# The lead-in of a fused linear-attention and gated-FFN kernel: wider state matmuls, other fillers, and w_in in six pieces

## Chip, cores, metric

The kernel runs on one core of a Trainium2 chip. The metric is the device time of one execution in microseconds; the median of ten runs is given where no other run is named. A single profiled execution gives the trace.

## What is computed

Linear attention with a decay per head over blocks of 64 positions, and then a feed-forward layer with a cosine gate on the 3,072 tokens that come out of it. Inputs are float32: q, k and v are [4, 8, 768, 64] (batch, heads, positions, head size), w_in is [512, 2048], w_out [2048, 512].

```python
for b in range(nb):                       # blocks of 64 positions
    intra = einsum('bhic,bhjc->bhij', qb, kb) * Dmask
    intra = einsum('bhij,bhjd->bhid', intra, vb)
    inter = einsum('bhid,bhde->bhie', qb * lam_pow, kv_state)
    out[:, :, sl] = intra + inter
    kv_state = lam_block * kv_state + einsum('bhsd,bhse->bhde', kb * rev_pow, vb)
x = out.transpose(0, 2, 1, 3).reshape(3072, 512)
h = x @ w_in
result = (h * cos(h)) @ w_out
```

## The kernel before

Positions are handled in tiles of 128 tokens, two tiles (a pair) at a time for attention. Tokens are grouped for the FFN in nine groups (`TILES`, 2 or 4 tiles each). For each group there are 16 blocks of 128 hidden columns: four matmuls per block (`hidden`, L707), a cosine on ScalarE (L713), a product on VectorE (L719); then a projection per tile of 16 matmuls, in groups of four (`project`, L751). While TensorE works through the FFN of one group, it does the attention of a later pair: scores (L420), state update (L432), values (L481), carried state (L509).

The first two pairs are different: two spans of 256 positions are loaded each by one DMA with the positions interleaved (`add_span`, L551). Per span, with two halves of four heads each: products of q and k with powers of lambda (L565, on VectorE, the second span's k on GpSimd), transposes on TensorE (L573) and copies on ScalarE (L576), scores (L584) masked by VectorE (L589), one state update per span (`update`, L592), whose two halves ScalarE copies into a block-diagonal bf16 tile (`update_out`, L602), values (L611), carried state (L617), and a copy of the result into xT (L625), which is the FFN's input.

In `update` TensorE makes, for each pair of heads p and each half s of the positions, two matmuls: head 2p into partitions 0 to 63 of one PSUM bank, head 2p+1 into 64 to 127 of another. That is 16 matmuls of 64x64 per span.

The order of work on every engine is set ahead of time by a list scheduler (`Planner`, L55): each task has an engine, an estimated duration, dependencies, a priority and a number of PSUM banks, and tasks are emitted in the planned order of starts. It sets only the order; at run time each engine goes through its instructions in that order and waits for semaphores. Loads go through two queues: SP (q, k, v, stores) and GpSimd (the two v spans, w_in, w_out, with a cast to bf16). Their order is the string `ORDER`; `i0` to `i4` are pieces of w_in, whose widths in blocks of 128 columns are `W_IN`, `o0` to `o3` are quarters of w_out. Piece 3 of w_in waits for the first masked scores of the second span (L307), and later loads wait for earlier ones (L793).

TensorE is kept busy in the lead-in by fillers that write a PSUM bank nobody reads: 94 matmuls of 64x32 at the very start (L841), and `keep_awake` (L830), called ahead of each planned TensorE task of the lead-in, which fills the planned gap with float32 matmuls on a zero tile:

```python
def keep_awake(us, at):
    cols = int((us - 0.06) * (1200.0 if at < 7.0 else 2400.0) / 4) // 64 * 64
    while cols > 0:
        n = min(cols, 4 * P)
        nc.tensor.matmul(idle_ps[:, :n], lhsT=blank[:, :P], rhs=blank[:, :n], start=True, stop=True)
        cols -= n
```

Of the kernel before, what the change touches and what calls it, by code (L numbers as in the profile page):

```python
# [10 lines left out]
F32 = mybir.dt.float32  # L11
# [20 lines left out]
VALUES_OUT = [("ACT", "ACT"), ("DVE", "ACT")]  # L32
STATE_OUT = [("ACT", "ACT"), ("ACT", "ACT")]
LATE = 30.0
AHEAD = 94
ORDER = "q0 k0 q1 k1 v0 v1 i0 i1 i2 i3 i4 o0 o1 o2 q4 q5 k4 k5 o3"

W_IN = [2, 2, 4, 4, 4]


class Task:
# [101 lines left out]
def kernel(  # L143
# [10 lines left out]
    nc = tc.nc  # L154
    B, H, S, D = q.shape
    P = 128
    NB = S // P
    NBLK = B * NB
    NP = H // 2
# [22 lines left out]
    def bank(i, shape, dt, name):  # L182
        return psum.tile(shape, dt, tag=f"bank{i}", bufs=1, name=name)
# [6 lines left out]
    ident = consts.tile([P, P], BF16)  # L190
# [20 lines left out]
    kv_bd = consts.tile([P, 2, NP, P], BF16)  # L211
# [29 lines left out]
    pl = Planner({**BUFS, "q_f": BUFS["ld"], "k_f": BUFS["ld"], "v_f": BUFS["ld"]})  # L241
# [3 lines left out]
    halves = [slice(i * D, (i + 1) * D) for i in range(2)]  # L245
# [20 lines left out]
    def start(queue, o, x, deps):  # L266
        i = queue.dma_start(out=o, in_=x)  # L267
        for d in deps:
            tc.add_manual_dep(i.ins, d.issue.ins.ins.name, mybir.DependencyInfo(
                mybir.DependencyClass.Sync, mybir.DependencyReason.DATA), reason="order of loads")  # L270
        return i
# [30 lines left out]
    def add_w(which, c, prio, deps=()):  # L302
        def emit(_):
            if which == "in":
                a, z = sum(W_IN[:c]) * P, sum(W_IN[:c + 1]) * P
                i = start(nc.gpsimd, w_in_sb[:, :, a:z], w_in_src[:, :, a:z], deps)
# [7 lines left out]

        part = W_IN[c] / 4 if which == "in" else 1.0
        early = which == "in" and c < 3
# [4 lines left out]
    T, So, Vo, d_t, Uo, Uo_sp = ({} for _ in range(6))  # L321
# [226 lines left out]
    spans, span_deps = [], []  # L548
    span_v = [consts.tile([P, H, 2, D], BF16, name=f"v_sp{x}") for x in range(SPANS)]

    def add_span(x):  # L551
        pa = lambda part: -1000.0 + 2 * x + part
        pv = lambda part: -990.0 + 2 * x + part
        cut = [slice(4 * hp, 4 * hp + 4) for hp in range(2)]
        us = {"DVE": 0.69, "POOL": 1.04}
        vec = {"DVE": nc.vector, "POOL": nc.gpsimd}
        L = {name: consts.tile([P, 2, H, D], BF16, name=f"{name}_sp{x}") for name in ("q", "k")}
# [32 lines left out]
                                        mask_sp.unsqueeze(1).to_broadcast([P, 2, 2, P]))  # L590

        def update(t):  # L592
            L["kv"] = [bank(i, [P, NP, D], F32, "ps_kv") for i in t.bank]
            rows = chunks[0][0]
            for p in range(NP):
                for s in range(2):
                    for i, h in enumerate(halves):
                        nc.tensor.matmul(L["kv"][i][h, p, :], lhsT=L["k"][rows, s, 2 * p + i, :], rhs=L["v"][rows, s, 2 * p + i, :],
                                         start=(p == 0 and s == 0), stop=True, skip_group_check=True)

        def update_out(_, h, e):
            (nc.scalar.copy if e == "ACT" else nc.vector.tensor_copy)(kv_bd[h, x, :, h], L["kv"][h.start // D][h])  # L602

        def values(task, hp):
            if hp == 0:
# [23 lines left out]
        so, kt, v_t = [[], []], [], [load_t["v_f", "sp", x]]  # L629
        for hp in range(2):  # L630
# [6 lines left out]
            for name, src in (("qT", a), ("kT", kt[hp])):  # L637
                e = OUTS[x][name][hp]
                t = pl.add("PE", MM(P, 4), [src, s_first if name == "kT" else None], partial(transposes, name=name, hp=hp), pa(-0.5 + 0.1 * hp), banks=1)
# [9 lines left out]
            if x and hp == 0:  # L649
                w_late.append(so[hp][0])  # L650

        u = pl.add("PE", 0.42, v_t + kt + [spans[0].get("carried")], update, pv(0.1), banks=2)
        Uo_sp[x] = [pl.add(e, 0.4 if e == "ACT" else 0.42, [u], partial(update_out, h=h, e=e), pv(0.1))
                    for h, e in zip(halves, STATE_OUT[x])]
        u.bank_frees = [[t] for t in Uo_sp[x]]
        span_deps.extend(v_t + kt)
        v0 = pl.add("PE", 0.35, so[0] + v_t + [spans[0].get("carried")], partial(values, hp=0), pv(0.2), banks=2)
        v1 = pl.add("PE", 0.35, [v0] + so[1], partial(values, hp=1), pv(0.25))
# [32 lines left out]
    def add_ffn(i):  # L691
# [4 lines left out]
        for f in range(KF):  # L696
            gate[f] = []
            blocks = [(0, 2), (2, 4)] if i == 0 and f < SPLIT else [(0, nb)]
            for b0, b1 in blocks:
# [16 lines left out]
                def gated(_, f=f, at=at, n=n):  # L716
                    if ("g", i) not in live:
# [3 lines left out]

                h = pl.add("PE", MM(n, 4), [x for m in range(n0 + b0, n0 + b1) for x in Vo[m]] + [w_t["in", next(c for c in range(len(W_IN)) if f < sum(W_IN[:c + 1]))]],
                           hidden, pr, banks=1)
# [59 lines left out]

    names = ORDER.split()
    for pr in range(SPANS, NBLK // 2):
# [18 lines left out]
    for x in range(SPANS):  # L804
        add_span(x)
# [22 lines left out]
    idle_ps = bank(idle.bank[0], [P, 4 * P], F32, "ps_idle")  # L828

    def keep_awake(us, at):  # L830

        cols = int((us - 0.06) * (1200.0 if at < 7.0 else 2400.0) / 4) // 64 * 64
        while cols > 0:
            n = min(cols, 4 * P)
            nc.tensor.matmul(idle_ps[:, :n], lhsT=blank[:, :P], rhs=blank[:, :n], start=True, stop=True)  # L835
            cols -= n

    for i in range(AHEAD):  # L841
        h = halves[i % 2]
        nc.tensor.matmul(idle_ps[h, :D // 2], lhsT=ident[h, :D], rhs=ident[h, :D // 2],
                         start=True, stop=True, skip_group_check=True)

    now = 4.2
    for t in plan:
        if t.eng == "PE" and t.start < lead_end.start + 1e-6:
            keep_awake(t.start - now, now)
            now = t.end  # L850
        if t.emit:
            t.ins = t.emit(t)
# [30 lines left out]
```

## Time and profile before

| | |
|---|---|
| median of 10 runs | 207.33 us (206.83 to 207.49) |
| profiled execution | 207.66 us |
| its span, first to last instruction | 206.0 us |
| TensorE: matmuls, busy | 2598, 198.9 us (97%) |
| VectorE, ScalarE, GpSimd busy | 55%, 58%, 31% |
| granted TensorE clock | 1.0 in all 40 slices |
| last span of the lead-in loaded (k of the second) | 11.04 us |
| first FFN matmul; FFN without pause from | 15.90 us; 17.44 us |

In the profile, PE stands for TensorE's matmuls, PEld for its weight loads, DVE for VectorE, ACT for ScalarE, POOL for GpSimd, SP for the queue of SyncE. L707 is line 707 of the kernel. A row of a timeline has the start, the duration and then the group of equal instructions; a bracket at its end gives the idle time before it and what ended that. A row of waits has the waiting group, what it waited for, then the total in us, how often, and the longest. A row by stretch has the stretch, its length, each engine's busy time with the number of its instructions, the granted clock, the share of the DMA engines and GB/s. In the list of DMA queues a row has packets, MB and the share of sixteen engines; q0 is GpSimd's queue, q1 that of SP, q8 and q14 carry instructions.

### The profile page before, as it was taken

What the parts mean: (1) busy time and instruction counts of PE and PEld (TensorE: products, weight loads), DVE (VectorE), ACT (ScalarE), POOL (GpSimd) and SP (SyncE); (2) the same over time, 40 slices, a digit from 0 to 9 for tenths busy, and PEclk for the clock granted to TensorE, in tenths of its full rate; (3) what the DMA queues carried; (4) which work ended last, traced back from release to release, by engine and by line L of the source; (5) the groups of instructions that cost most, each with busy time, mean ns of one, the idle gap of its engine ahead of it and who ended that gap; (6) DMA issues with size and microseconds to landing.
All of it is one profiled execution on the core that took longest, in us unless ns stands there. A gap on an engine that the chain in (4) does not pass through costs nothing.

```text
span 206.0 us, 6189 instructions
## 1 busy us (share of the span) xinstructions
PE 198.9 (97%) x2598; PEld 121.1 (59%) x2598; DVE 113.3 (55%) x221; ACT 119.0 (58%) x232; POOL 63.9 (31%) x84
## 2 busy tenths in 40 slices
PE   6999999999999999999999989999999999999993
PEld 5767444547747848666658756755454444444463
DVE  2688774256943947558467664735688444444001
ACT  5878772128837868466649476654778555354120
POOL 5856004056053364617254442524500000000000
PEclk9999999999999999999999999999999999999999
DMA  4999999998899999999996988988900110111112
GB/s 123 315 192 206 205 192 210 176 206 217 192 254 147 283 218 259 226 188 252 207 279 148 254 170 184 225 200 195 202 0 3 54 51 0 51 51 54 51 73 80
DMA packets 96379, 33.95 MB, mean 165 GB/s; under 512 B 84320, under 2 KB 93408, under 8 KB 96352
## 3 DMA queue, kind: packets, MB, share of 16 engines
q1 hardware_dynamic: 89376, 28.78, 62.1%
q0 software_dynamic: 6832, 4.72, 15.7%
q8 instruction: 20, 0.33, 0.6%
q10 hardware_dynamic: 144, 0.07, 0.1%
q14 instruction: 7, 0.06, 0.1%
HBM read 27.27 MB, written 6.29 MB: 163 GB/s over the span
## 4 chain that ended last, share of the span: by engine, by line
PE 77%; DMA 15%; SPq 3%; POOL 2%; issue 1%; DVE 1%; ACT 0%; POOLq 0%; ACTq 0%
PE ps_f L751 35%; PE ps_h L707 34%; DMA w_out_sb<-in_moe_w_out_dram 6%; DMA v_f<-in_v_dram 3%; DMA sp_f<-in_k_dram 3%; SPq L267 3%; PE ps_o L481 2%; DMA k_f<-in_k_dram 2%; PE ps_kv L432 2%; PE ps_o L509 1%; PE ps_s L420 1%; POOL w_in_sb L267 1%; POOL k_sp L565 1%; DVE v_s L350 0%; POOL w_out_sb L267 0%
## 5 line engine op out<-in xcount | busy, mean ns | idle before, releaser
L719 DVE TENSOR_TENSOR g<-ps_h,cos 128x256 bf16<-128x256 f32 (+1 forms) x148 | 72.9, 503 | 52.0 <-ACT cos L713 51.0
L713 ACT ACTIVATE cos<-ps_h,halfpi 128x256 f32<-128x256 f32 (+1 forms) x148 | 75.7, 538 | 32.3 <-PE ps_h L707 32.0
L751 PE MATMUL ps_f<-w_out_sb,g 128*128 128x512 bf16 (+2 forms) x416 | 92.4, 363 | 0.8 <-issue 0.8
L707 PE MATMUL ps_h<-xT,w_in_sb 128*128 128x256 bf16 (+1 forms) x592 | 91.8, 304 | 0.0
L707 PEld LDWEIGHTS <-w_in_sb 128*128 128x128 bf16 x592 | 57.3, 98 | 30.6 <-DVE xT L517 0.4
L751 PEld LDWEIGHTS <-g 128*128 128x128 bf16 x416 | 38.3, 98 | 36.7 <-issue 1.2
L765 ACT COPY o_sb<-ps_f 128x512 f32<-128x512 f32 (+1 forms) x24 | 13.8, 573 | 30.2 <-PE ps_f L751 30.2
L342 POOL TENSOR_TENSOR qk<-q_f,q_scale 128x512 bf16<-128x512 f32 x19 | 19.6, 1043 | 36.7 <-DMA q_f<-in_q_dram 28.7
L350 POOL TENSOR_TENSOR v_s<-v_f,v_scale 128x512 bf16<-128x512 f32 x19 | 19.7, 1042 | 19.5 <-DMA v_f<-in_v_dram 17.2
L517 ACT CAST xT<-ps_o 128x512 bf16<-128x512 f32 x19 | 10.2, 588 | 11.5 <-PE ps_o L509 9.0
L425 DVE TENSOR_TENSOR s_m<-ps_s,mask 128x512 bf16<-128x512 f32 x20 | 12.9, 683 | 3.3 <-PE ps_s L420 3.0
L346 POOL CAST qk<-k_f 128x512 bf16<-128x512 f32 x18 | 10.9, 611 | 8.1 <-DMA k_f<-in_k_dram 8.0
L438 DVE TENSOR_TENSOR sum<-sum,ps_kv 128x512 f32<-128x512 f32 x15 | 10.2, 682 | 0.8
L443 ACT CAST S<-sum 128x512 bf16<-128x512 f32 x15 | 9.0, 615 | 0.8 <-DVE sum L438 0.7
L481 PEld LDWEIGHTS <-v_s 64*64 64x64 bf16 x320 | 4.3, 106 | 5.0 <-issue 4.4
L481 PE MATMUL ps_o<-s_m,v_s 64*64 64x64 bf16 x320 | 6.4, 197 | 0.5
L765 DVE COPY o_sb<-ps_f 128x256 f32<-128x256 f32 (+1 forms) x2 | 0.7, 358 | 11.2 <-PE ps_f L751 11.2
L835 PE MATMUL ps_idle<-blank 128*128 128x192 f32 (+4 forms) x16 | 6.3, 499 | 0.0
L589 DVE TENSOR_TENSOR s_m_sp<-ps_s,mask_sp 128x512 bf16<-128x512 f32 x8 | 5.0, 683 | 0.9 <-PE ps_s L584 0.9
L432 PE MATMUL ps_kv<-v_s,qk 64*64 64x64 bf16 x288 | 4.7, 194 | 0.3 <-DVE v_s L350 0.3
L681 POOL CAST S<-sum 128x512 bf16<-128x512 f32 x1 | 0.6, 606 | 13.4 <-DVE sum L678 13.4
L509 PE MATMUL ps_o<-qkT,S 64*64 64x64 bf16 x304 | 4.6, 193 | 0.0
(70 smaller groups left out, 83.5 us busy)
## 6 DMA issues: line engine op xcount, KB each, us to landing
q_f<-in_q_dram SPq DMA_DIRECT2D x20, 256.0 KB, 3.5
k_f<-in_k_dram SPq DMA_DIRECT2D x20, 256.0 KB, 4.2
v_f<-in_v_dram SPq DMA_DIRECT2D x20, 256.0 KB, 4.7
out_dram<-o_sb SPq DMA_DIRECT2D x19, 256.0 KB, 2.3
w_out_sb<-in_moe_w_out_dram POOLq DMA_DIRECT2D x4, 512.0 KB, 11.3
w_in_sb<-in_moe_w_in_dram POOLq DMA_DIRECT2D x3, 512.0 KB, 8.6
out_dram<-o_sb SPq DMA_DIRECT2D x9, 128.0 KB, 3.6
sp_f<-in_q_dram SPq DMA_DIRECT2D x2, 512.0 KB, 5.7
```

Source lines behind the costliest of these rows:

```text
L342: vec[e].tensor_mul(new_qk()[:, 0, :, s], live.pop(("q_f", 2 * pr + s)), q_scale[:, c, :].unsqueeze(2).to_broadcast([P, H, D]))
L346: (nc.scalar.copy if early else nc.gpsimd.tensor_copy)(new_qk()[:, 1, :, s], live.pop(("k_f", 2 * pr + s)))
L350: vec[e].tensor_mul(live["v_s", 2 * pr + s], live.pop(("v_f", 2 * pr + s)), v_scale[:, c, :].unsqueeze(2).to_broadcast([P, H, D]))
L425: nc.vector.tensor_mul(t, live["s", pr][s], mask.unsqueeze(1).to_broadcast([P, H, D]))
L438: nc.vector.tensor_add(new, live["sum", pr, 0] if half else live["sum", pr - 1, 1], live["kv", pr][half])
L481: yield lambda h=h: nc.tensor.matmul(o[halves[h % 2], h // 2, m], lhsT=live["v_s", n0 + s][m, h, :], rhs=live["s_m", n0 + s][m, h, :], sta ...
L517: (nc.vector.tensor_copy if e == "DVE" else nc.scalar.copy)(live["xT", tile_i][:, :, j * P:(j + 1) * P], live.pop(("o", n0 + s)))
L707: nc.tensor.matmul(t[:, :n], lhsT=w_in_sb[:, kd, f * P:(f + 1) * P], rhs=live["xT", i][:, kd, at], start=(kd == 0), stop=(kd == KD - 1))
L713: nc.scalar.activation(c[:, :n], live["h", i, f, at.start][:, :n], AF.Sin, bias=halfpi)
L719: nc.vector.tensor_mul(live["g", i][:, f, at], live.pop(("h", i, f, at.start))[:, :n], live.pop(("c", i, f, at.start))[:, :n])
L751: nc.tensor.matmul(live["f", i, j, piece][:, :width], lhsT=live["g", i][:, f, j * P:(j + 1) * P], rhs=w_out_sb[:, f, part], start=(f == 0) ...
L765: (nc.scalar.copy if eng == "ACT" else nc.vector.tensor_copy)(o[:, :width], live["f", i, j, piece][:, :width])
```

## The change

The state update of a span takes both heads of a pair in one matmul: 128 columns of k by 128 columns of v, of which only the two 64x64 blocks on the diagonal are read. There are 8 matmuls per span instead of 16, and one PSUM bank instead of two. The 94 small fillers at the start are gone; the first planned gap is now counted from 1.6 us on and filled with float32 matmuls. Planned gaps under 0.6 us get one bf16 matmul of 512 columns on the identity tile, or none if under 0.25 us. w_in comes in six pieces of 2, 2, 2, 4, 4 and 2 blocks instead of five of 2, 2, 4, 4 and 4.

```diff
-AHEAD = 94
-ORDER = "q0 k0 q1 k1 v0 v1 i0 i1 i2 i3 i4 o0 o1 o2 q4 q5 k4 k5 o3"
-W_IN = [2, 2, 4, 4, 4]
+ORDER = "q0 k0 q1 k1 v0 v1 i0 i1 i2 i3 i4 i5 o0 o1 o2 q4 q5 k4 k5 o3"
+W_IN = [2, 2, 2, 4, 4, 2]
...
-            L["kv"] = [bank(i, [P, NP, D], F32, "ps_kv") for i in t.bank]
+            L["kv"] = bank(t.bank[0], [P, NP, P], F32, "ps_kv")
...
-                    for i, h in enumerate(halves):
-                        nc.tensor.matmul(L["kv"][i][h, p, :], lhsT=L["k"][rows, s, 2 * p + i, :], rhs=L["v"][rows, s, 2 * p + i, :],
-                                         start=(p == 0 and s == 0), stop=True, skip_group_check=True)
+                    nc.tensor.matmul(L["kv"][:, p, :], lhsT=L["k"][rows, s, 2 * p:2 * p + 2, :], rhs=L["v"][rows, s, 2 * p:2 * p + 2, :],
+                                     start=(p == 0 and s == 0), stop=True, skip_group_check=True)
...
-            (nc.scalar.copy if e == "ACT" else nc.vector.tensor_copy)(kv_bd[h, x, :, h], L["kv"][h.start // D][h])
+            (nc.scalar.copy if e == "ACT" else nc.vector.tensor_copy)(kv_bd[h, x, :, h], L["kv"][h, :, h])
...
-        u = pl.add("PE", 0.42, v_t + kt + [spans[0].get("carried")], update, pv(0.1), banks=2)
+        u = pl.add("PE", 0.42, v_t + kt + [spans[0].get("carried")], update, pv(0.1), banks=1)
...
-        u.bank_frees = [[t] for t in Uo_sp[x]]
+        u.bank_frees = [Uo_sp[x]]
...
+        if us < 0.6:
+            if us > 0.25:
+                nc.tensor.matmul(idle_ps, lhsT=ident, rhs=ident.unsqueeze(1).to_broadcast([P, 4, P]), start=True, stop=True)
+            return
...
-    for i in range(AHEAD):
-        h = halves[i % 2]
-        nc.tensor.matmul(idle_ps[h, :D // 2], lhsT=ident[h, :D], rhs=ident[h, :D // 2],
-                         start=True, stop=True, skip_group_check=True)
-    now = 4.2
+    now = 1.6
...
-            keep_awake(t.start - now, now)
+            keep_awake((t.start - now) * 0.95 if now < 2.0 else t.start - now, now)
```

In the order of instructions, VectorE's and ScalarE's are unchanged. TensorE's tasks keep their order, and its program goes from 5,226 to 5,000 instructions (weight loads, matmuls, waits; a float32 matmul counts as four). On SP, among the loads and stores after the first four stores, one q load, one k load and two DMA transposes trade places with stores.

## The prediction

> **What bounds the kernel now.** I read the page's busy shares first, then the waits of TensorE (PE), then its timeline in the lead-in (0 to 17.44 us), then the chain of work around the only long unexplained gap.
>
> ```profile
> PE 198.9 (97%) x2598; PEld 121.1 (59%) x2598; DVE 113.3 (55%) x221; ACT 119.0 (58%) x232; POOL 63.9 (31%) x84
> q8 instruction: 20, 0.33, 0.6%
> ```
>
> PE is busy for 198.9 of 206.0 us, no other engine above 58%. The second line (packets, MB, share) is the program's own text: 20 packets of 16 KB. The waits of PE are four:
>
> ```profile
> PE ps_idle L843 <- POOL ident masks.py:199: 1.6, 1, 1.6
> PE ps_f L751 <- issue: 0.8, 1, 0.8
> PE ps_t L573 <- POOL k_sp L565: 0.3, 1, 0.3
> PE ps_kv L432 <- DVE v_s L350: 0.3, 1, 0.3
> ```
>
> So after the lead-in every microsecond of PE work is a microsecond of the kernel, except 0.28 us at 44.3 (the last row, where v has only just been loaded) and the row called "issue". The timeline of PE in the lead-in (start, duration, then the instruction group):
>
> ```profile
> 9.77 0.42 PE L584 MATMUL ps_s<-qT_sp,kT_sp 64*64 64x128 bf16 x16
> ...
> 12.31 0.40 PE L573 MATMUL ps_t<-ident,k_sp 128*128 128x128 bf16 x4 [0.30 <-POOL k_sp L565]
> 12.63 0.44 PE L598 MATMUL ps_kv<-v_sp,k_sp 64*64 64x64 bf16 x16
> 13.00 0.49 PE L835 MATMUL ps_idle<-blank 128*128 128x128 f32 x2
> 13.42 0.42 PE L584 MATMUL ps_s<-qT_sp,kT_sp 64*64 64x128 bf16 x16
> ...
> 15.24 0.35 PE L598 MATMUL ps_kv<-v_sp,k_sp 64*64 64x64 bf16 x12
> ...
> 15.90 1.03 PE L707 MATMUL ps_h<-xT,w_in_sb 128*128 128x256 bf16 x8
> 16.86 0.42 PE L611 MATMUL ps_o<-s_m_sp,v_sp 64*64 64x128 bf16 x16
> ```
>
> Up to 12.31 PE waits for POOL, which waits for the second k span, landed at 11.04. Everything PE does before that has a cover. From 12.31 on PE is gapless.
>
> The "issue" gap, in the chain of work, and what the instruction queue did just before (transfers of 118.25 to 119.00 us):
>
> ```profile
> 120.09 0.21 PE ps_f L751
> 120.31 0.77 issue
> 121.08 0.82 PE ps_f L751 x3
> ```
>
> ```profile
> q8 instruction: 1, 0.02, 10.6%
> ```
>
> The gap stands inside a group of four L751 matmuls that share their wait, so no data explains it. The busy time by stretch tells where it stands in PE's program (matmuls and weight loads up to 6.30 and 119.95 us):
>
> ```profile
> 0.00:6.30 6.30, 4.68 (x98) 3.62 (x98) 2.13 (x8) 3.81 (x8) 3.07 (x15) 1.00 0.58 164
> 0.00:119.95 119.95, 117.20 (x1751) 77.78 (x1751) 75.78 (x155) 75.69 (x157) 51.89 (x71) 1.00 1.05 214
> ```
>
> The first packet of q8 ran at 6.3, after 196 PE instructions; the gap came after 3,502. With the some 20 waits and drains that leave no record that is 13 lines of 256 instructions (3,328), and 20 x 256 is about PE's 5,226. So PE ran out of instructions: the packet that ran at 118.31 to 119.58 came late, and PE went on 1.5 us after its end.
>
> **Part by part.** The sum is made against the profiled execution: 207.66 us, a span of 206.0 and 1.66 around it, 0.33 above the median of the runs, 207.33. I carry only the difference over to the median.
>
> Fillers (the 94 small ones gone, two 512s and a 256 on the zero tile ahead, one 512-column bf16 on ident in place of four f32 ones): before 12.31 they are worth nothing, since 12.31 is set by the load at 11.04 and two POOL products. PE may reach kT about 0.5 us sooner (the f32 filler at 7.70 lasts until 8.44), and then DVE is the cover: its scores cannot begin before its q products end at 10.87. If the clock stays open, 0. The filler at 13.00 is after the cover: two f32 passes of 128 took 0.42 from start to scores; a bf16 512 is 512/128 x 56 ns = 0.22 plus about 0.09 for the change of tile shape = 0.31. So -0.11.
>
> State matmuls: 16 of 64x64 become 8 of 64 rows x 128 columns, streaming 128 columns instead of 64. In the trace the 64x64 ones run in pairs, 31 ns a pair: 8 pairs are 0.25, and with entry and exit 12.63 to 13.00 is 0.37. For 8 with 128 columns the nearest row is the transposes, 56 ns apart when the clock is open: 66 + 6 x 56 = 0.40 to the eighth, then 0.15 to the next shape: 0.55. In the first span +0.18; less the filler's 0.11, scores move from 13.42 to 13.49 (kT ends on ACT at 13.32, so PE sets it). In the second span the old update has the shape of its neighbours and slips between them: 15.20 to 15.49, with values already started at 15.41. The new one changes shape twice: 0.15 + 0.40 + 0.15 = 0.70, about 0.42 more. Of that 0.08 is hidden, because the FFN at 15.90 waited for xT (ACT, 15.84). So 0.07 + 0.42 - 0.08, about **+0.42** at 16.86 and at 17.44. Bounds: +0.1 if two of the new matmuls overlap, +0.6 if a 128-column load is not hidden. The Trainium skill (TensorEngine Tiling (Array Packing), "Key Properties") says that a change of tiling mode drains the engine; the trace prices it at 0.15 against 0.05 in one shape. By instruction count alone, at the skill's floor of 25 ns each (TensorE: Matmul & The Clock Gate, "Wait — 56ns, not 53.3ns?"), 16 fewer matmuls would be a gain of 0.4 instead; the trace's pairs start 3 ns apart, so I take the row.
>
> At 44.3 PE waits 0.28 for v_s. It now comes 0.42 later, so the wait goes and **+0.14** remains, if v comes no later. Bank use: one instead of two, both state copies now read one bank; ACT issues them one after the other anyway, 0.
>
> w_in in six pieces: POOL issues one more, at 0.77, so the three w_out issues move from 16.40 to about 17.15; their data's turn came at 24.24 or later: hidden by 7 us. Pieces of two took 1.34 (landings 15.27, 16.61), of four 2.35 to 2.76, so two more small ones cost 0 to 0.15 on the way to the w_out landing at 29.36 that releases q and then v: within PE's 0.14 of room. The early set ends at about 17.9; the next piece, issued at 14.87, can move data from about 17 (w_out's last: issued 33.78, moving after 35.5), so no hole, by under 1 us. Column blocks 6 to 9 now land near 20.4 and are first used near 22.2. Beyond: SP's stores of two tiles pass ahead of one q and one k load near 54 to 58; stores take 0.5 to 1 us to issue, PE shows no wait for such loads, POOL had slack: 0, at most 0.3.
>
> Instruction lines: PE's program shrinks by 226 instructions (5,226 to 5,000), so every later boundary falls 226 later in the old program, which is 30 before an old one. The gap at 120.3 goes: 119.93 to 121.08 is 1.15, of which 0.22 is the normal step, so **-0.93**. But other boundaries come close together. I took, for each new boundary, when PE's sequencer can reach it ([...]held by its last wait) and when PE needs the next line. Old windows were never under 6.19 us except that the one that starved had 5.8 without its gap. New ones: 13.6 to 19.4 (5.8 us); 113.0 to 117.9 (4.8, since scores, updates and values burn 256 instructions in 1.6 us); 137.3 to 141.8 (4.4). A line needs, measured: 0.7 to 4.0 us until its packet starts (4.0 when three loads are queued ahead), 0.9 to 1.3 for it, 1.5 after it.
> - 137.3: the old packet asked for at the same point ran 140.16 to 141.10, so PE gets it at 142.6 against 141.75: **+0.85** (0 to 1.5).
> - 113.0: one store and one load are ahead, that load lands at 115.67; packet to 116.7, usable 118.2 against 118.0: **+0.2** (0 to 1.9, the latter with the 3.97 us of the packet asked for 1.3 us later).
> - 13.6: old packet to 18.18, usable 19.7, needed at 19.4 + 0.42: 0.
>
> Here the Trainium skill speaks against me: Runtime: NRT & Kernel Launch, "Instruction fetch mechanics", gives PE room for 2,048 instructions and calls the crossing of a block mostly hidden. By it this whole term is 0, the change is the +0.14, and the gap stays unexplained. With eight blocks held, 20 refills of 256 for 5,226 instructions would not fit; the row decides.
>
> Sum: +0.14 - 0.93 + 0.2 + 0.85 = **+0.26**, so 207.6.
>
> **The rivals.**
> A, forecast (0.36): starvation moves from one place to another; 207.6, within 0.2% (0.41 us, about what a measurement of this kernel can tell from no change).
> B, starvation gets worse (0.26): the line needed at 117.9 sits behind loads as its old neighbour did. For: the window is the tightest but one, beside a packet that waited 3.97. Against: only one load is queued when it is asked for. Price 0.14 - 0.93 + 1.9 + 0.85 = +1.96: 209.3. It decides when the new gaps exceed 0.79 together; slower by 0.2% from 1.2.
> C, the lines fit (0.26): packets near 113 and 137 start in the 1 us that several took: 0.14 - 0.93 = -0.8, 206.5, or 206.4 with the state matmuls overlapped.
> D, the clock stays shut (0.12): the transposes' spacing goes from 107 ns to 56 at 8.4; until then PE was gapless from 1.6. The skill (clock-gate page, "What's actually happening") asks for a busy window of 3.4 us, free-running. The new fillers end near 5.9 and leave gaps to 12.3. If no window counts, PE is at half speed to about 18: the 5.1 us from 12.30 to 17.44 grow by 1 to 3.5, giving 208.5 to 211. It costs only from the point where slow PE work outlasts 12.3.
> That the change doesn't do what it says: 8 matmuls do replace 16, but PE time rises.
>
> **Numbers.** Faster by over 0.2%: C, 0.26. Same: 0.36. Slower: B and D, 0.38. Range 206.5 to 209.3: C and B are in; left out are about 0.08 below and 0.1 above, D's far part. The likeliest case alone: 207.0 to 207.75.
>
> **What would show it.** Right: the L573 transposes at 56 ns before 12.3; L596 as 8 matmuls with 0.40 from first to last; the first steady FFN group near 17.86; no wait at 44.3; no issue gap in L751 near 120, one near 141. Wrong: a gap over 1 us near 118 (B), none at all (C), 107 ns after 12.3 (D), or a w_in wait in L705 between 19 and 23.

## The result and the profile after

| | before | after |
|---|---|---|
| median | 207.42 us (206.57 to 209.72, 50 runs, the first ten among them) | 206.30 us (205.72 to 207.63, 15 runs) |
| profiled execution, its span | 207.66, 206.0 us | 206.38, 204.7 us |
| k of the second span landed | 11.04 us | 10.30 us |
| FFN without pause from | 17.44 us | 17.16 us |
| third matmul of the state update near 44 us | 44.34 us | 44.17 us |

The ratio is 0.9944 with an interval of [0.9928, 0.9961]: 0.56% faster, about 1.16 us. The forecast was 207.6 with a range from 206.5, so the time is just outside it on the fast side. It is rival C (the lines fit) with a further gain in the lead-in that no case had.

The page of the kernel after, its busy row and its row of instruction packets (packets, MB, share):

```profile
PE 198.2 (97%) x2485; PEld 118.0 (58%) x2485; DVE 113.4 (55%) x221; ACT 119.2 (58%) x232; POOL 64.5 (32%) x85
q8 instruction: 19, 0.31, 0.6%
```

TensorE is as full as before; one packet of instructions is gone. The waits of PE after:

```profile
PE ps_idle L837 <- DVE blank L209: 1.6, 1, 1.6
PE ps_t L572 <- DVE q_sp L564: 0.5, 1, 0.5
PE ps_kv L431 <- DVE v_s L349: 0.3, 1, 0.3
PE ps_t L572 <- POOL k_sp L564: 0.2, 1, 0.2
```

The "issue" row of 0.8 us is gone, and no new one has come. The wait for v, which I had down as used up, is still there. The one for q_sp is new; it ends at 6.72, ahead of the load of k, and costs nothing. PE's timeline around the old gap, after:

```profile
118.81 1.04 PE L705 MATMUL ps_h<-xT,w_in_sb 128*128 128x256 bf16 x8
119.68 1.03 PE L749 MATMUL ps_f<-w_out_sb,g 128*128 128x512 bf16 x4
120.55 1.04 PE L705 MATMUL ps_h<-xT,w_in_sb 128*128 128x256 bf16 x8
```

The group of four is whole: no bracket, and the next group begins 0.87 later. PE's timeline in the lead-in, after:

```profile
11.57 0.40 PE L572 MATMUL ps_t<-ident,k_sp 128*128 128x128 bf16 x4 [0.23 <-POOL k_sp L564]
11.90 0.62 PE L596 MATMUL ps_kv<-v_sp,k_sp 64*128 64x128 bf16 x8
12.45 0.39 PE L833 MATMUL ps_idle<-ident 128*128 128x512 bf16 x1
12.77 0.42 PE L583 MATMUL ps_s<-qT_sp,kT_sp 64*64 64x128 bf16 x16
...
14.70 0.62 PE L596 MATMUL ps_kv<-v_sp,k_sp 64*128 64x128 bf16 x8
15.25 0.42 PE L609 MATMUL ps_o<-s_m_sp,v_sp 64*64 64x128 bf16 x16
15.60 1.05 PE L705 MATMUL ps_h<-xT,w_in_sb 128*128 128x256 bf16 x8
...
17.16 1.04 PE L705 MATMUL ps_h<-xT,w_in_sb 128*128 128x256 bf16 x8
```

Two things stand in it. The state update as a block does cost what was expected: from the transposes to the FFN without pause it is 17.16 - 11.57 = 5.59 us, before 17.44 - 12.31 = 5.13, so +0.46. But the whole block starts 0.74 sooner, because k has landed at 10.30 instead of 11.04. So the FFN comes 0.28 sooner, where +0.42 later was forecast.

By the same instruction in both traces: at 105 us after is 0.17 ahead of before (105.44 against 105.61), at 129 us 1.20 ahead (128.53 against 129.73), at the end 1.28. So 0.17 comes from the lead-in and 1.03 from the stretch around the gap near 120, of which the gap itself is 0.93.

### The profile page after: what moved, and what is told of

Same layout as the page of the kernel before. It is cut to its first block, busy times and chain, and to the rows that moved or that the text cites. A ratio compares the mean times of both kernels' runs of the same rounds, so it can differ in the third digit from the quotient of the medians.

```text
span 204.7 us, 5964 instructions
## 1 busy us (share of the span) xinstructions
PE 198.2 (97%) x2485; PEld 118.0 (58%) x2485; DVE 113.4 (55%) x221; ACT 119.2 (58%) x232; POOL 64.5 (32%) x85
## 4 chain that ended last, share of the span: by engine, by line
PE 77%; DMA 14%; SPq 3%; POOL 2%; issue 1%; DVE 1%; ACT 0%; POOLq 0%; ACTq 0%
PE ps_f L749 36%; PE ps_h L705 34%; DMA w_out_sb<-in_moe_w_out_dram 6%; DMA v_f<-in_v_dram 3%; DMA sp_f<-in_k_dram 3%; SPq L266 3%; PE ps_o L480 2%; DMA k_f<-in_k_dram 2%; PE ps_kv L431 2%; PE ps_o L508 1%; PE ps_s L419 1%; POOL w_in_sb L266 1%; POOL k_sp L564 1%; DVE v_s L349 0%; POOL w_out_sb L266 0%
## 5 line engine op out<-in xcount | busy, mean ns | idle before, releaser
L763 DVE COPY o_sb<-ps_f 128x256 f32<-128x256 f32 (+1 forms) x2 | 0.7, 358 | 11.2 <-PE ps_f L749 11.2
L837 PE MATMUL ps_idle<-blank 128*128 128x512 f32 (+2 forms) x8 | 5.4, 824 | 1.6 <-DVE blank L209 1.6
L266 POOL DMA_DIRECT2D w_in_sb<-in_moe_w_in_dram x6 | 4.6, 774 | 1.7 <-DVE s_m_sp L588 1.7
```

Of the source, the lines that this page charges most:

```text
L763: (nc.scalar.copy if eng == "ACT" else nc.vector.tensor_copy)(o[:, :width], live["f", i, j, piece][:, :width])
```

## The experiments

Two theories were to be told apart for the gain, with a question on each part of the change.

- The lines' theory: the gap near 120 depends only on where PE's program is cut into lines of 256 instructions. Any change of the program's length ahead of it can remove it, and none of the change's stated parts has to do with it. The rival: the new order of loads (w_in) keeps the queues free at that point.
- The packet's theory, formed after the first runs: the 94 small fillers make PE ask for its second line at once. That packet of 16 KB then runs at 6.3 us in the midst of the loads of the spans, on one DMA engine, and k of the second span lands later by as much. The rival: the order of the loads or their issue sets when k lands, which the fillers don't touch.

### Lines as in after, nothing else changed

```diff
-AHEAD = 94
+AHEAD = 109
```

30 instructions more, so the lines of before begin where those of after do.

> The kernel before with 109 small fillers ahead instead of 94 and nothing else: TensorE's program is 30 instructions longer, so from the lead-in on every 256-instruction line begins at the same place of the work as in the changed kernel. Theory I (the gain is the instruction gap at 120 us, set by where lines begin): no issue gap in L751 near 120, 0.9 us faster, 206.4 to 206.6. Rival L (the gain is made in the lead-in, by fillers, state matmuls or w_in, and the gap is a matter of one profile): within 0.2 us of before, gap present or not.

Measured: 206.63 us, ratio 0.9957 [0.9939, 0.9975]. PE's timeline:

```profile
119.25 1.04 PE L707 MATMUL ps_h<-xT,w_in_sb 128*128 128x256 bf16 x8
120.13 1.03 PE L751 MATMUL ps_f<-w_out_sb,g 128*128 128x512 bf16 x4
```

No gap. Fifteen useless matmuls more make the kernel 0.43% faster; the gap's 0.93 us is 0.45% of its time. This one edit, which has none of the change's parts, gives about three quarters of its gain.

### After, with the lines put back as in before

```diff
+    for i in range(117):
+        h = halves[i % 2]
+        nc.tensor.matmul(idle_ps[h, :D // 2], lhsT=ident[h, :D], rhs=ident[h, :D // 2],
+                         start=True, stop=True, skip_group_check=True)
-    now = 1.6
+    now = 4.7
```

> The changed kernel with 117 small fillers put ahead (and the float32 filler shortened to start after them), so that TensorE's program has 5,226 instructions again and its lines begin where those of the kernel before do. Theory I: the issue gap of about 0.8 to 1.0 us is back near 120 us and the time is 207.1 to 207.4. Rival L: 206.3 as the changed kernel, if the fillers ahead do not matter. A second theory, P (the first instruction packet of 16 KB delays the span loads by its own 0.9 us): with the early packet back, the second span of k lands at about 11.0 us as before and not at 10.3, and the FFN starts 0.7 us later than in the changed kernel.

Measured: 208.31 us, 1.0029 [1.0007, 1.0051]. The gap is back:

```profile
120.93 0.38 PE L749 MATMUL ps_f<-w_out_sb,g 128*128 128x512 bf16 x1
121.78 0.82 PE L749 MATMUL ps_f<-w_out_sb,g 128*128 128x512 bf16 x3 [0.47 <-issue]
```

From one matmul of the group to the next it is 0.85 instead of 0.22 us. But that is 0.63, and the kernel lost 0.85% against after, some 1.8 us. The rest is in the lead-in: k landed at 11.28 instead of 10.30, and the state update near 44 ran at 45.35 instead of 44.17, 1.18 later. 1.18 + 0.63 = 1.81. This set off the packet's theory.

### The state matmuls alone, on before

AHEAD is 110 here, so that the program keeps its 5,226 instructions.

```diff
-AHEAD = 94
+AHEAD = 110
...
-                    for i, h in enumerate(halves):
-                        nc.tensor.matmul(L["kv"][i][h, p, :], lhsT=L["k"][rows, s, 2 * p + i, :], rhs=L["v"][rows, s, 2 * p + i, :],
+                    nc.tensor.matmul(L["kv"][:, p, :], lhsT=L["k"][rows, s, 2 * p:2 * p + 2, :], rhs=L["v"][rows, s, 2 * p:2 * p + 2, :],
...
```

> The kernel before with the changed state matmuls alone (8 of 64 rows by 128 columns per span), and 110 small fillers ahead so that the length of the program and its lines stay as before. Step of the prediction: FFN without pause starts 0.4 us later (17.85), the wait for v at 44.3 takes 0.28 of it, so 0.1 to 0.15 us slower than before, gap at 120 still there. Rival (fewer instructions are cheaper): 0.2 to 0.4 us faster.

Measured: 207.88 us, 1.0014 [0.9994, 1.0035], not told from no change. PE's timeline, at the second span's k and where the FFN runs without pause:

```profile
12.24 0.40 PE L573 MATMUL ps_t<-ident,k_sp 128*128 128x128 bf16 x4 [0.31 <-POOL k_sp L565]
...
17.92 0.49 PE L706 MATMUL ps_h<-xT,w_in_sb 128*128 128x256 bf16 x3
```

The FFN without pause comes 0.48 later than before; at 44 it is level (44.33 against 44.34), since the wait for v took it up; and the gap near 120 was 1.56 instead of 1.15, which is the whole of this profile's loss.

### w_in in six pieces alone, on before

```diff
-ORDER = "q0 k0 q1 k1 v0 v1 i0 i1 i2 i3 i4 o0 o1 o2 q4 q5 k4 k5 o3"
-W_IN = [2, 2, 4, 4, 4]
+ORDER = "q0 k0 q1 k1 v0 v1 i0 i1 i2 i3 i4 i5 o0 o1 o2 q4 q5 k4 k5 o3"
+W_IN = [2, 2, 2, 4, 4, 2]
```

> The kernel before with w_in in six pieces alone. Step of the prediction: the second w_out quarter lands 0 to 0.15 us later, v at 43.6 to 43.7, time within 0.2 us of before, gap at 120 still there. What the changed kernel's trace suggests instead: the w_out quarter lands 0.8 us later, at 30.2, the q loads after it are issued 0.8 us later, and v still comes at 43.3 to 44.4, so 0 to 0.8 us slower.

Measured: 208.34 us, 1.0035 [1.0015, 1.0056]: slower, and the gap near 120 is still there (0.84). So the loads' new order doesn't remove it, and the rival to the lines' theory falls. By stretch (the last three columns are the granted clock, the share of the DMA engines and GB/s), of this kernel:

```profile
16.00:17.00 1.00, 0.99 (x10) 0.73 (x8) 0.90 (x2) 0.94 (x3) 1.00 (x2) 1.00 0.67 93
17.00:18.00 1.00, 1.00 (x25) 0.86 (x25) 0.81 (x2) 0.80 (x3) 1.00 (x2) 1.00 0.97 122
```

of the kernel after:

```profile
16.00:17.00 1.00, 1.00 (x24) 0.67 (x23) 0.34 (x2) 0.86 (x3) 1.00 (x2) 1.00 1.27 170
17.00:18.00 1.00, 1.00 (x12) 0.92 (x13) 1.00 (x3) 0.80 (x3) 1.00 (x3) 1.00 1.22 196
```

and of the kernel after with the old w_in (the next experiment):

```profile
16.00:17.00 1.00, 1.00 (x25) 0.69 (x24) 0.58 (x2) 0.82 (x2) 1.00 (x3) 1.00 1.21 208
17.00:18.00 1.00, 1.00 (x11) 0.90 (x10) 0.78 (x2) 0.97 (x3) 0.67 (x1) 1.00 1.27 205
```

With old widths the DMA engines move 208 and 205 GB/s (before itself 212 and 209). With six pieces alone it is 93 and 122: the three early pieces are through before the fourth, which waits for the first masked scores of the second span, has anything to move. Short of 206 that is 113 + 84, about 0.95 us of transfer lost. In the kernel after, whose scores come earlier, it is 36 + 10, about 0.2 us. The second quarter of w_out lands at 30.62 here, 1.26 later than before, and the state update near 44 runs 0.42 later. (Part of the hole may be the lead-in's: in this execution the FFN without pause comes 0.15 later than before, and the fourth piece was issued at 15.02 instead of 14.87.) Where the rest of this kernel's 0.35% goes its one profile does not tell: that execution took 207.61 us, as fast as before.

### After with the old w_in, twice

```diff
-ORDER = "q0 k0 q1 k1 v0 v1 i0 i1 i2 i3 i4 i5 o0 o1 o2 q4 q5 k4 k5 o3"
-W_IN = [2, 2, 2, 4, 4, 2]
+ORDER = "q0 k0 q1 k1 v0 v1 i0 i1 i2 i3 i4 o0 o1 o2 q4 q5 k4 k5 o3"
+W_IN = [2, 2, 4, 4, 4]
```

> The changed kernel with w_in in the old five pieces. Theory V (both kernels wait at 44 us for v, whose load hangs on the w_out quarter, and the two extra pieces cost that chain 0.8 us): w_out's second quarter lands near 28.8, v by 42.9, the wait of TensorE at 44 shrinks to 0 to 0.1, and the time is 0.2 to 0.3 us below the changed kernel, 206.0. Rival (pieces do not matter for the end, as the prediction had it): 206.3, wait at 44 unchanged. No issue gap near 120 in either case, since TensorE's program is the same.

> The changed kernel with the old five pieces of w_in, once more, on the chip of the two kernels beside it, as the one that they are compared with. 205.8; v within 0.2 us of TensorE at 43.4.

Measured: 205.83 us, 0.9909 [0.9875, 0.9944], and 206.06 us, 0.9936 [0.9917, 0.9955]. w_out's second quarter lands at 29.05 and 29.37 (after: 30.20), and the third matmul of the state update near 44 runs at 43.41 and 43.49 instead of 44.17. PE's timeline of the first of them:

```profile
43.23 0.62 PE L431 MATMUL ps_kv<-v_s,qk 64*64 64x64 bf16 x32
```

The row holds all 32 matmuls, without a wait for v of 0.15 us or more. In the profiles 0.6 us are saved against after; in the medians 0.2 to 0.5 us, and the intervals overlap with after's. The second of the two ran beside after with the old short fillers (below), which has w_in in six pieces: six runs of each, 205.82 to 206.22 against 206.18 to 206.71. So w_in in six pieces brings no gain here and probably costs a little.

### After with the old state matmuls

The opposite of the third edit above, on after; 5,032 instructions.

> The changed kernel with the old state matmuls (16 of 64x64 per span). Theory V: FFN without pause starts 0.4 us earlier, near 16.75, but the wait for v at 44 takes all of it, so the time is that of the changed kernel, 206.3, unless lines of instructions, which begin 32 instructions earlier, starve somewhere else. Rival S (the 8 wide matmuls are the gain): 0.3 us slower or more, 206.6 and above, with no issue gap. Rival T (their 0.4 us is lost to the end): 205.9.

Measured: 206.20 us, 0.9921 [0.9891, 0.9951]. PE's timeline:

```profile
16.45 0.38 PE L706 MATMUL ps_h<-xT,w_in_sb 128*128 128x256 bf16 x2
17.52 2.34 PE L706 MATMUL ps_h<-xT,w_in_sb 128*128 128x256 bf16 x19 [0.69 <-issue]
```

The FFN without pause would begin at 16.45, 0.71 sooner than in after; the first step at 11.35 to there is 5.10 against 5.59. But 32 instructions more put a boundary of lines at once behind the lead-in, and PE waits 0.69 for it. The old state matmuls save 0.49 us of TensorE's time in the lead-in, and the line takes it back. In this profile v is there in time all the same (w_out's second quarter lands at 29.47 instead of 30.20): the third matmul near 44 us runs at 43.70, 0.47 sooner than in after. The medians of the two, 206.20 and 206.30, are not told apart.

### Fewer fillers on before

```diff
-AHEAD = 94
+AHEAD = 38
```

```diff
-AHEAD = 94
+AHEAD = 66
```

> The kernel before with 38 small fillers ahead instead of 94, 112 instructions fewer. By the prediction's way of reckoning windows the tightest line is one of 3.7 us near 127 us, so an issue gap of 1 to 2 us there and 207.5 to 208.5. If what decides is only where a packet meets queued loads, no gap need be there and the time is 206.4. Theory P: the first instruction packet runs after the span loads, so the second k span lands near 10.3, not 11.0, and the FFN starts without pause near 16.8.

> The kernel before with 66 small fillers ahead, 56 instructions fewer. No line has a window under 8.5 us, so by every theory of lines there is no issue gap: 206.4 to 206.6. If the gain of the first run was something other than the gap, 207.4. Theory P: the first packet is asked for near 9 us, so k of the second span lands between 10.3 and 11.0.

Measured: 207.84 us, 1.0009 [0.9995, 1.0023] with 38, and 207.01 us, 0.9968 [0.9945, 0.9990] with 66. In both the second line's packet comes later (at 14.52 and 11.64) and k lands at 10.10 and 10.03. Neither has the gap near 120, and the first none near 127 either, where the reckoning of windows had one. But they lose in the lead-in what k gained, one of them most of it, the other more. The transposes come 107 ns apart at first and 56 ns apart only from some point between 9.5 and 11.4 us, and PE is then later than k. (The granted clock in the rows by stretch is 1.00 all along; only the spacing shows this.) That the few fillers cause it is not shown: in w_in alone, whose PE rows up to 7.70 us are those of before, the spacing changes between 9.62 and 9.98 us, in before between 7.70 and 8.52, and with 109 fillers not before 9.30. With 38 fillers a boundary of lines also stops PE in the values of the second span:

```profile
16.07 0.28 PE L611 MATMUL ps_o<-s_m_sp,v_sp 64*64 64x128 bf16 x3
17.02 0.36 PE L611 MATMUL ps_o<-s_m_sp,v_sp 64*64 64x128 bf16 x11 [0.67 <-issue]
```

### The short fillers of before, in after

```diff
-        if us < 0.6:
-            if us > 0.25:
-                nc.tensor.matmul(idle_ps, lhsT=ident, rhs=ident.unsqueeze(1).to_broadcast([P, 4, P]), start=True, stop=True)
-            return
```

> The changed kernel with the old float32 fillers in the short gaps (64, 192, 192, 192 and 128 columns) in place of one bf16 matmul of 512. Step of the prediction: worth 0.11 us at the filler ahead of the second span's scores and nothing before. What the runs so far suggest: float32 fillers double while the clock is still shut, and with a clock that opens after 8.5 us TensorE falls behind the loads, so the FFN starts 0.3 to 0.8 us later than in the changed kernel in such an execution, and the median is 0.1 to 0.4 us slower. Rival (fillers are worth nothing): 206.3, FFN without pause from 17.2 in every case.

Measured: 206.37 us, 0.9952 [0.9934, 0.9970], level with after; FFN without pause from 17.08 against 17.16. In the time of the kernel the kind of the short fillers can't be seen. In the lead-in of its profile it can: from the transposes at 11.40 to 17.08 it is 5.68 us, where after and both kernels with the old w_in have 5.58 to 5.59. That is 0.09 to 0.10 for the bf16 filler; the wait for v at 44 us (0.33 here) covers it.

### The parts that seemed best together

After with the old w_in, and the old state matmuls in the second span only; 5,016 instructions.

```diff
...
+            if x:
+                L["kv"] = [bank(i, [P, NP, D], F32, "ps_kv") for i in t.bank]
+                for p in range(NP):
+                    for s in range(2):
+                        for i, h in enumerate(halves):
+                            nc.tensor.matmul(L["kv"][i][h, p, :], lhsT=L["k"][rows, s, 2 * p + i, :], rhs=L["v"][rows, s, 2 * p + i, :],
+                                             start=(p == 0 and s == 0), stop=True, skip_group_check=True)
+                return
...
```

> The changed kernel with the old five pieces of w_in, and the old state matmuls in the second span alone, where they stand between neighbours of their own shape. Theory: FFN without pause 0.35 to 0.4 us sooner than with the wide ones (16.4 to 16.8); the second line boundary of TensorE comes 16 instructions later than with old matmuls in both spans, about 0.9 us, so the line is just there and no issue gap stands in the FFN near 17; the v load then sets the end again, and the time is 0 to 0.3 us below the same kernel with wide ones, 205.5 to 205.8. Rival: the line is still late and the gap takes the 0.4 back, 205.9.

Measured: 205.91 us, 0.9929 [0.9912, 0.9946]. PE's timeline:

```profile
16.58 1.26 PE L713 MATMUL ps_h<-xT,w_in_sb 128*128 128x256 bf16 x10
18.29 1.90 PE L713 MATMUL ps_h<-xT,w_in_sb 128*128 128x256 bf16 x13 [0.46 <-issue]
```

Again the FFN starts sooner (16.58), and again a line comes late and takes most of it. This kernel and after with the old w_in (205.83 and 206.06) are the fastest of the study; they are not told apart, nor surely from after.

### The packet that delays a load

What bears on the packet's theory is read from the traces of the kernels above. The list of DMA queues from 6.0 to 6.6 us, before:

```profile
q1 hardware_dynamic: 404, 0.20, 111.0%
q8 instruction: 1, 0.02, 9.2%
```

9.2% of sixteen engines in 0.6 us is 0.88 us of one engine, while q1 (SP's queue) holds them all with the spans' loads. From 5.5 to 9 us after there is no row of q8:

```profile
q1 hardware_dynamic: 2402, 1.21, 114.8%
```

And from 10.0 to 11.2 us, before, when q1 should be done:

```profile
q0 software_dynamic: 820, 0.21, 173.6%
q1 hardware_dynamic: 30, 0.01, 4.1%
```

30 packets of 512 bytes, some 15 KB, are a tail of q1 that takes 4.1% of 16 x 1.2 us, 0.79 us of one engine; that is about what the 16 KB of instructions took. After has no row of q1 in this stretch. In the chain of work the load of k, before and then after:

```profile
4.09 6.95 DMA sp_f<-in_k_dram
```

```profile
4.33 5.98 DMA sp_f<-in_k_dram
```

It takes 0.97 us less from issue to landing. Over all thirteen kernels: with a packet at 6.3 to 6.6 us (before and the runs with at least 94 fillers ahead, five) k lands at 10.97 to 11.28; without one there (eight) at 9.97 to 10.30. The two groups don't touch, and the two runs with 38 and 66 fillers, which differ from before in nothing else, are in the second. From issue to landing the load takes 5.97 to 5.99 us in all eight and 6.85 to 7.21 in the five: 0.87 to 1.23 more, for a packet of 0.88 to 0.96.

The trace also keeps the completions of this load one by one, sixteen of them, as many as there are DMA engines. In before fifteen come from 9.45 to 10.08 and the last alone at 11.04; in the other four with an early packet fifteen come by 10.06 to 10.11 and the last 0.86 to 1.22 later. In the eight without one no completion is more than 0.15 behind the one before it. So one of the sixteen shares is late and the others are not. That it is the share of the engine that carried the packet is inferred from size and time; the records don't name the engine. Why the delay grows with the packet's start (0.86 for 6.26 us, 1.22 for 6.59) was not tried.

### Where the lines end

The count of PE's records (each weight load with its matmul as two, each wait as one) bears on all gaps called "issue" above. The first instruction behind the gap is number 3,521 in the four kernels of 5,226 instructions that have it, and number 450 with 38 fillers, in after with the old state matmuls and in the best parts: 193 or 194 above a multiple of 256 in all seven. PE goes on 1.25 to 1.60 us after the end of the packet each time. With the packets taken in order, the first for the line from about number 450, there are 234 other such places in the thirteen traces: there PE comes 1.43 us or more after the packet's end and shows no gap. So a gap is a line that PE needed sooner than some 1.5 us after its packet; in after the closest are 1.79 (at 19.12 us) and 1.85 (at 117.62).

### All runs in one account

Two numbers of each profile, the third matmul of the state update near 44 us and the step across the old gap (0.22 is the step without one), against before. "Account" is the sum of the two differences; the last column is the difference of the profiled executions' times.

| kernel | at 44 | step near 120 | account | measured |
|---|---|---|---|---|
| before | 44.34 | 1.15 | | |
| after | 44.17 | 0.22 | -1.10 | -1.28 |
| before, 109 fillers | 44.62 | 0.22 | -0.65 | -0.76 |
| before, 66 fillers | 44.20 | 0.22 | -1.07 | -1.13 |
| before, 38 fillers | 45.28 | 0.22 | +0.01 | +0.30 |
| after, 117 fillers | 45.35 | 0.85 | +0.71 | +0.62 |
| before, state matmuls | 44.33 | 1.56 | +0.40 | +0.45 |
| before, w_in | 44.76 | 0.84 | +0.11 | -0.05 |
| after, old w_in | 43.41 and 43.49 | 0.22 | -1.86 and -1.78 | -1.96 and -1.84 |
| after, old state matmuls | 43.70 | 0.22 | -1.57 | -1.70 |
| after, old short fillers | 44.39 | 0.22 | -0.88 | -1.02 |
| best parts | 43.61 | 0.22 | -1.66 | -1.75 |

Two places account for every profiled execution to within 0.3 us, all but one within 0.2.

## Why the prediction was wrong

**The step that failed is the new starvation**: "137.3: the old packet asked for at the same point ran 140.16 to 141.10, so PE gets it at 142.6 against 141.75: +0.85", and with it "113.0: ... +0.2". Both are 0. The list of DMA queues after, from 135.5 to 136.0 us:

```profile
q8 instruction: 1, 0.02, 11.7%
```

This packet ran at 135.79 to 136.72, 4.4 us before the time that I gave it, and its line was needed at 140.56, 1.2 before the forecast 141.75, since the whole kernel is ahead by then. Put back by these 1.2 us it starts at 136.98, still before 137.3, the earliest time at which I had let it be asked for. The other ran at 114.89 to 115.77 and was needed at 117.62 (both needs by the count of instructions). The third, "13.6: ... 0", held: packet at 16.36 to 17.33, and no wait in the lead-in. In the run with 109 fillers, which has the same lines, the two ran at 115.53 and 136.10. I had taken the moment of the request from PE's sequencer, held by its last wait, and the delay behind it from one old packet. A rule drawn from so few packets did not survive when the lines moved; used once more, near 127 with 38 fillers, it failed again. What lets a line be asked for, and when, stays open. Without this term my sum was -0.79 on the profiled execution, which is rival C; the 1.05 us are most of the miss of 1.54 (+0.26 against -1.28). Of the rest 0.31 is in the lead-in (-0.17 at 44 us against +0.14), 0.18 is not placed.

**"The gap at 120.3 goes: ... -0.93"** was right, in place and size, and for the reason given: moving the lines alone does it (0.9957), putting them back brings it back. The Trainium skill's rule that such crossings are mostly hidden (Runtime: NRT & Kernel Launch, "Instruction fetch mechanics") holds for all 19 packets of after and for most elsewhere (234 of 241 crossings show no gap), but one exception near 120 costs 0.6 to 1.3 us (the step less 0.22), as much as all of this change.

**"Before 12.31 they are worth nothing, since 12.31 is set by the load at 11.04"** was wrong. I took the load's landing as given. The small fillers were what made it late, through a packet which the prediction itself names ("the first packet of q8 ran at 6.3, after 196 PE instructions") and never set beside the load that ran at that time. In after k lands 0.74 us sooner, and so the transposes come 0.74 sooner.

**State matmuls "+0.42"** was right, in its parts too: 0.46 from the two traces, 0.55 from the update alone on before (5.68 against 5.13; forecast without the filler's -0.11: 0.52), 0.49 from its undoing in after. The filler's -0.11 is 0.09 to 0.10. "It now comes 0.42 later, so the wait goes" was right in the run with that edit alone (44.33, no wait). In after the whole lead-in is 0.28 ahead instead of 0.42 behind, and the wait did not go.

**w_in "0 to 0.15", "so no hole, by under 1 us"** was wrong in size. The hole is there: about 0.95 us of transfer in the run with w_in alone, about 0.2 in after. w_out's second quarter came 0.84 later in after and 1.26 in w_in alone. In after it hides most of the 0.74 that k gained: with the old widths PE reaches the third matmul near 44 us some 0.7 sooner. So at 44.3 it is -0.17 where I had +0.14, and about -0.9 in the two runs without this part of the change (-0.93 and -0.85).

**Rival D**, the clock: the transposes are 56 ns apart from 8.09 on after, before the work that k's load releases. It did not happen. A later change of the spacing is in the traces of before with 38, 66 and 109 fillers and of w_in alone (above); what brings it on stays open.

## What to carry to other kernels

Where an engine's program is long, look for a gap with no data behind it and count the instructions up to it. If it falls on the edge of a line, a few instructions more or fewer ahead of it can decide about half a per cent, as here, and any edit, meant to or not, shifts all edges at once; so compare variants at the same program length, or read the gaps before believing a ratio. And count instructions as transfers: here a burst of cheap fillers at the start brought the next line's packet just when the first loads ran, and the load that the lead-in waits for came later by about the packet's own time.

## What was not expected of the hardware

- One packet of 16 KB of instructions (0.88 us of one DMA engine) delays a load that is spread over all sixteen by about its own time or a little more: it lands at 9.97 to 10.30 us without it, at 10.97 to 11.28 with it, and fifteen of its sixteen completions are on time.
- PE can run out of instructions in the lead-in as well: 0.69 us in after with the old state matmuls, 0.46 in the best parts, 0.67 with 38 fillers; 32 and 16 instructions more than in after are enough for the first two.
- The transposes go from 107 to 56 ns apart between 7.70 and 8.52 us in before and between 9.62 and 9.98 in w_in alone, with equal PE rows up to 7.70. What sets the moment stays open.
- The gap near 120 differs among kernels of the same lines: 0.84, 0.85, 1.15 and 1.56 us a step, with its packet at 118.94, 119.37, 118.31 and 118.63. Where in the queue it waits, and for what, was not tried.
